# Pacing early weight loads, moving a quarter of the tail products, chaining late loads on one queue, and merging stores, in a two-branch attention kernel

## The chip, the cores and the metric

The kernel runs on one core of one Trainium2 chip. The metric is device time in microseconds (us). The kernel before took 2483.39 us (median of 4 runs, 2479.60 to 2484.12).

The names used below: TensorE does matrix products into PSUM, VectorE, ScalarE and GpSimd work on vectors, and SyncE here only issues DMA transfers. GpSimd issues some too. The profile calls TensorE's products PE, its weight loads PEld, and SyncE's queue SPq. SBUF is the memory that holds the weights loaded here, PSUM the one that the products are written to; a bank is one of the kernel's buffers there (eight in the tail). The granted clock is the share of full speed that TensorE was allowed (0.50 is half clock), the DMA share the mean busy share of the 16 DMA engines. A transfer is issued by a queue and lands when its completion is signalled. The drain is the end of the sliding branch, where TensorE runs short of work.

## The reference, cut to what matters

```python
x = A_x                                            # 2048 x 640
g = sigmoid((x * gate_w).sum(-1, keepdims=True))
a = sliding_window_attention(x, wqkv, wo)          # 32 heads of 20, window 256
# b: recurrent; 64 segments of 32 tokens, 8 memory tokens, 32 heads of 192
for s in range(64):
    h = concat(mem, x_s)                           # 40 x 640
    q, k, v = h @ Wq, h @ Wk, h @ Wv               # each 640 x 6144
    o = softmax(mask(q k^T)) v @ Wo
    mem, out_s = o[:8], o[8:]
return g * a + (1 - g) * b
```

The recurrent branch is sequential in `mem`, so it can't be spread. The queries, keys and values of a segment's own 32 tokens do not depend on `mem`. For the last eight of them the kernel computes these for all segments at once: these are the dense "tail" products. They run between the two branches.

## The kernel before

The matrices of the recurrent branch are cut into 84 units: 64 stay in SBUF (29 loaded early, 32 late, 3 last) and 20 are streamed in every segment from a packed copy in DRAM. The kernel records operations in a small list scheduler, which then emits instructions in the order of its own simulated clock. That clock decides only the order of each queue; the profile shows what an instruction then waited for: an input block's load that the scheduler counts as 500 ns held a product for 46.63 us.

```python
# (cut) early work of the sliding branch: to the scheduler these are free transfers
units  = [lambda sc, u=u: sc.op("DMA", 500, lambda: weights.load_resident(pre, u, nc.sync)) for u in early]
units += [lambda sc, u=u: sc.op("DMA", 500, lambda: weights.pack(u, nc.sync)) for u in streamed]
...
    # (cut) one output-weight unit is four transfers of 64 rows x 1280 bytes
    for r in range(2):
        i, b = divmod(2 * c + r, 3)
        for a in range(2):
            engine.dma_start(dst[64*a:64*a+64, r*D:(r+1)*D], self.Wo[8*g+2*i+a, 64*b:64*b+64, :])
...
# (cut) main
branch_A(..., units)                                  # sliding branch
for u in late: weights.load_resident(post, u, nc.gpsimd)      # 32 units at once
tail_projections(tc, weights, xTb, xbqk, xbv)         # dense products, 8 PSUM banks
for u in last: weights.load_resident(end, u, nc.gpsimd)
branch_B(...)                                         # recurrent branch
mix_out(...)
```

## Time and profile before

| stage | from, to (us) | length |
|---|---|---|
| sliding branch, with its stall | 0 to 435.8 | 435.8 |
| query and key products of the tail | 435.8 to 557.8 | 122.0 |
| value products of the tail | 557.8 to 615.2 | 57.4 |
| gap to the first recurrent product | 615.2 to 622.6 | 7.4 |
| first recurrent segment | 622.6 to 653.7 | 31.1 |
| the other 63 segments and the output mix | 653.7 to 2483.5 | 1829.8 |

The borders are the starts of the first and last products of a stage (so a stage's last product is cut off by its own length, some 0.3 us), and for a segment the copy of the new memory.

In the list of what TensorE waited for (us in total, times, longest us):

```profile
PE p_m L247 <- DMA a_xt<-in_A_x_dram: 59.1, 2, 46.6
...
PE t_psum L576 <- DVE t_qk L583: 12.5, 1, 12.5
```

The first is the stall for an input block. The second is TensorE's wait for the 26.66 us store of the chain.

### The profile page before, as it was taken

How to read it: one execution, taken by the hardware profiler on the slowest of the kernel's cores; microseconds unless marked ns; L12 is line 12 of the kernel's file. 1: busy time of each engine (PE TensorE's matmuls, PEld its weight loads, DVE VectorE, ACT ScalarE, POOL GpSimd, SP SyncE). 2: the span in 40 equal slices, each digit the busy share in tenths (PEclk: the TensorE clock that was granted, in tenths of full speed). 3: DMA queues.
4: the chain of work that ended last, by engine and by line, in shares of the span. 5: the costliest groups of instructions: out<-in, count | busy, mean ns of one | idle time of the engine just before them, and what ended most of it. 6: DMA issues, size and time to landing. Idle time of an engine off the chain costs nothing.

```text
span 2483.5 us, 112898 instructions
## 1 busy us (share of the span) xinstructions
PE 2129.7 (86%) x49059; PEld 1521.8 (61%) x49093; DVE 1133.4 (46%) x3942; ACT 1047.4 (42%) x2385; POOL 745.7 (30%) x2097
## 2 busy tenths in 40 slices
PE   2799997798888888888888888888888888888885
PEld 2477765795566665556666665565666666666664
DVE  2588885232344443334444444343443443444434
ACT  1588886122344333334433443333333333343333
POOL 2255554501322222222222222222222222222220
PEclk7899997899899999999999999999999999999997
DMA  9200000955788888878888887888887888888888
GB/s 327 61 21 27 27 19 9 298 148 140 246 276 272 272 275 265 255 246 267 274 270 272 278 270 253 259 280 264 264 267 251 264 266 280 270 273 263 269 260 244
DMA packets 298288, 561.55 MB, mean 226 GB/s; under 512 B 104568, under 2 KB 116864, under 8 KB 297792
## 3 DMA queue, kind: packets, MB, share of 16 engines
q1 hardware_dynamic: 273712, 513.01, 64.8%
q0 software_dynamic: 19808, 37.07, 5.2%
q8 instruction: 385, 6.31, 1.0%
q10 hardware_dynamic: 4272, 4.26, 0.6%
q14 instruction: 111, 0.91, 0.1%
HBM read 524.83 MB, written 36.51 MB: 226 GB/s over the span
## 4 chain that ended last, share of the span: by engine, by line
PE 56%; DMA 36%; ACT 3%; issue 2%; SPq 1%; DVE 1%; POOL 0%; ACTq 0%; DVEq 0%; POOLq 0%
DMA t_w<-w_packed 31%; PE ps_k L737 8%; PE ps_q L737 8%; PE ps_o L907 7%; PE ps_v L737 6%; PE t_psum L576 4%; PE p_s L326 3%; PE p_m L281 3%; PE ps_pv L883 2%; PE tr_k L752 2%; PE p_o L410 2%; PE S_ps L809 1%; PE t_psv L593 1%; PE p_st L326 1%; PE tr_q L752 1%
## 5 line engine op out<-in xcount | busy, mean ns | idle before, releaser
L737 PEld LDWEIGHTS <-t_hT 128*32 128x32 bf16 x15360 | 380.2, 98 | 286.7 <-issue 57.9
L907 PE MATMUL ps_o<-t_OT,t_w 128*128 128x40 bf16 x7040 | 289.3, 180 | 120.3 <-DMA t_w<-w_packed 111.9
L907 PE MATMUL ps_o<-t_OT,w_o 128*128 128x40 bf16 x8320 | 320.8, 180 | 47.2 <-ACT t_OT L888 45.2
L907 PEld LDWEIGHTS <-t_w 128*128 128x128 bf16 x7040 | 225.5, 96 | 141.7 <-DMA t_w<-w_packed 138.9
L907 PEld LDWEIGHTS <-w_o 128*128 128x128 bf16 x8320 | 267.1, 96 | 58.2 <-issue 48.4
L784 POOL COPY t_K<-t_xqk 128x64 bf16<-128x64 bf16 x256 | 60.9, 238 | 769.0 <-PE S_ps L809 763.6
L356 DVE CUSTOM_DVE_ANT_0 a_junk<-p_s,a_mask 128x384 bf16<-128x384 f32 (+2 forms) x512 | 253.5, 528 | 45.0 <-PE p_st L326 32.9
L386 ACT ACTIVATE a_pt<-p_st 128x384 bf16<-128x384 f32 (+2 forms) x512 | 220.4, 474 | 89.9 <-PE p_st L326 81.1
L737 PE MATMUL ps_v<-w_v,t_hT 128*32 128x384 bf16 x4864 | 252.9, 336 | 0.6 <-issue 0.6
L888 ACT CAST t_OT<-ps_pv 128x480 bf16<-128x480 f32 x256 | 143.2, 559 | 246.3 <-PE ps_pv L883 242.5
L737 PE MATMUL ps_q<-w_q,t_hT 128*32 128x384 bf16 x4096 | 220.0, 336 | 20.5 <-DVE t_hT L918 20.2
L775 DVE COPY t_K<-tr_k 128x256 bf16<-128x256 bf16 x256 | 74.6, 291 | 339.5 <-PE tr_k L752 339.1
L737 PE MATMUL ps_k<-w_k,t_hT 128*32 128x384 bf16 x4096 | 223.2, 339 | 0.6 <-issue 0.6
L742 ACT CAST t_tok<-ps_k 128x384 bf16<-128x384 f32 x256 | 122.7, 479 | 208.3 <-PE ps_k L737 208.3
L761 ACT COPY b_QT<-tr_q 128x384 bf16<-128x384 bf16 x256 | 123.3, 481 | 179.4 <-PE tr_q L752 179.4
L866 DVE TENSOR_TENSOR t_PTx<-PT_ps,mk_x 128x320 bf16<-128x320 f32 x256 | 125.9, 492 | 153.3 <-PE PT_ps L859 153.3
L394 POOL TENSOR_SCALAR_AFFINE_SELECT a_pt<-a_pt 128x512 bf16<-128x512 bf16 x240 | 148.0, 639 | 124.5 <-ACT a_pt L386 123.5
L742 ACT CAST t_tok<-ps_q 128x384 bf16<-128x384 f32 x256 | 122.6, 479 | 138.0 <-PE ps_q L737 137.6
L819 DVE TENSOR_REDUCE sm_mx<-S_ps 128x4 f32<-128x160 f32 x256 | 82.2, 321 | 204.4 <-PE S_ps L809 203.3
L742 ACT CAST t_vtok<-ps_v 128x384 bf16<-128x384 f32 x256 | 122.7, 479 | 103.0 <-PE ps_v L737 102.8
L697 POOL DMA_DIRECT2D t_xqk<-xbqk x256 | 137.4, 537 | 87.0 <-POOL b_QT L765 40.9
L326 PE MATMUL p_st<-a_qa,a_k 64*128 64x128 bf16 x1440 | 150.7, 224 | 10.6 <-ACT a_pt L386 7.3
(140 smaller groups left out, 4059.1 us busy)
## 6 DMA issues: line engine op xcount, KB each, us to landing
t_w<-w_packed SPq DMA_DIRECT2D x704, 320.0 KB, 4.2
t_w<-w_packed SPq DMA_DIRECT2D x576, 384.0 KB, 4.4
xbqk<-t_qk SPq DMA_DIRECT2D x16, 768.0 KB, 5.3
t_xqk<-xbqk POOLq DMA_DIRECT2D x256, 48.0 KB, 3.6
w_v<-in_B_Wv_dram POOLq DMA_DIRECT2D x19, 384.0 KB, 8.3
w_q<-in_B_Wq_dram SPq DMA_DIRECT2D x16, 384.0 KB, 7.3
xbv<-t_vt SPq DMA_DIRECT2D x64, 96.0 KB, 1.8
t_xv<-xbv POOLq DMA_DIRECT2D x128, 48.0 KB, 4.0
```

Of the source, the lines that this page charges most:

```text
L326: nc.tensor.matmul(T(out)[:, i * P:(i + 1) * P], lhsT=b if keys_first else a, rhs=a if keys_first else b, start=True, stop=True, tile_posi ...
L356: sc.op("DVE", 135 + n / 0.96, lambda: nc.vector.tensor_tensor_reduce(out=T(junk)[:, 0:n], in0=T(s)[:, 0:n], in1=mask[:, NKB * P - n:], op ...
L386: sc.op("ACT", act_ns(n), lambda: nc.scalar.activation(out=T(pt)[:, h % 4, 0:n], in_=T(s)[:, 0:n], func=ACT.Exp), reads=[s], writes=[pt])
L394: nc.gpsimd.affine_select(out=v, in_=v, compare_op=op, fill=0.0, base=0, pattern=[[0, 4], [sign, P]], channel_multiplier=-sign)
L576: nc.tensor.matmul(pt[:, bb, :], lhsT=ws[ki][kt][:, c:c + P], rhs=xTb[:, kt, t * P:(t + 1) * P], start=(kt == 0), stop=(kt == KT - 1))
L697: sc.op("DMA", 500, lambda: nc.gpsimd.dma_start(tile_of(qk)[:].rearrange("p i b t -> p (i b t)"), xbqk[s, :, g].rearrange("p i c -> p (i c ...
L737: nc.tensor.matmul(t[32 * j:32 * j + 32, 0:384], lhsT=tile_of(hT)[:, kt, :], rhs=w[:, j * 384:(j + 1) * 384], start=(kt == kts[0]), stop=( ...
L742: sc.op("ACT", act(384), lambda: nc.scalar.copy(tile_of(tok)[:], b["tile"][:, 0:384]), reads=[b], writes=[tok])
L761: nc.scalar.copy(dst, tq["tile"][:].rearrange("p b (j t) -> p b j t", t=SEG))
L866: nc.vector.tensor_tensor(out=tile_of(dst)[:], in0=PT["tile"][:, i, :, :].unsqueeze(2).to_broadcast([P, 2, 4, L]), in1=mk.unsqueeze(1).uns ...
L888: sc.op("ACT", act(480), lambda: nc.scalar.copy(tile_of(OT)[:].rearrange("p b j l -> p (b j l)"), o["tile"][:, 0:480]), reads=[o], writes= ...
L907: nc.tensor.matmul(t[:, dt * L:(dt + 1) * L], lhsT=w[:, r * D + dt * P:r * D + (dt + 1) * P], rhs=OT["tile"][:, b, i, :], start=(g == 0 an ...
```

## The change

The intent: stop the early loads from blocking the input blocks; fill the drain of the sliding branch with dense products; keep the late loads from crowding out the stores; and issue fewer, larger stores.

```diff
-    early, late, last = weights.resident[:29], weights.resident[29:-3], weights.resident[-3:]
+    early, late, last = weights.resident[:23], weights.resident[23:-2], weights.resident[-2:]
-    units = [... sc.op("DMA", 500, load_resident(pre, u, nc.sync)) for u in early]
-    units += [... sc.op("DMA", 500, pack(u, nc.sync)) for u in streamed]
+    units = [lambda sc, after, u=u: pack(sc, after, u) for u in streamed]          # now "SP", 1300
+    units += [lambda sc, after, u=u: sc.op("SP", 1300, load_resident(pre, u, nc.sync), after=after) for u in early]
 # in the sliding branch's loop: each unit follows a TensorE operation
-                units.pop(0)(sc)
+                units.pop(0)(sc, [o for o in sc.ops[-8:] if o["eng"] == "PE"][-1:])
 # after the sliding branch's last operation has been recorded
+        tail(sc)              # tail_qk of the first quarter, PSUM tag "m" (2 banks)
 # the tail has its own schedule now; late loads are chained on SyncE
+        for n, u in enumerate(late):
+            loads[u] = sc.op("SP", 1300, load_resident(post, u, nc.sync), after=[loads[late[n-1]]] if n else [])
+        for g in range(1, 4): tail_qk(...)
+        for g in range(4):    tail_v(...)
 # value stores: one for four PSUM tiles
-                    nc.sync.dma_start(xbv[h:h+2, tt*P:(tt+1)*P, :]..., vt[:])          # 64 x 96 KB
+        sc.op("SP", 1500, nc.sync.dma_start(xbv[8*g:8*g+8, tt*P:(tt+1)*P, :]..., view))  # 16 x 384 KB
 # (cut) the two "last" units load on SyncE inside the recurrent branch
```

More of the change, by code (lines that the diff above doesn't have):

```diff
@@ L137, in act_ns, with branch_A @@
     return 105 + n / 1.2
-def branch_A(tc, x, wqkv, wo, gate_w, spread_x, ga_dram, omg_dram, units, W=256, HA=32):
+def branch_A(tc, x, wqkv, wo, gate_w, spread_x, ga_dram, omg_dram, units, tail, W=256, HA=32):
     nc = tc.nc
@@ L159, in branch_A @@
               "rl": (2, [P, HH], FP32), "aT": (1, [P, KT, P], BF), "ga": (1, [P, D], BF), "zc": (1, col, FP32), "ez": (1, col, FP32),
-              "den": (1, col, FP32), "gcol": (4, col, FP32)}
+              "den": (1, col, FP32), "gcol": (4, col, FP32), "ts": (2, [P, P // MEM, 2, 12, MEM], BF), "w": (1, [P, 4 * 384], BF)}
         for i in range(2):
@@ L489, in branch_A @@
         for u in units:
-            u(sc)
+            u(sc, [])
         for _, u in queue:
             u()
+        tail(sc)
         with tc.manual_schedule():
@@ L552, in get, with tail_weights @@
         return t
-def tail_projections(tc, weights, xTb, xbqk, xbv):
+def tail_weights(sc, nc, weights, g, kinds, loads):
+    ws = {}
+    for u in [(k, g, kt) for k in kinds for kt in range(KT)]:
+        b = None
+        if u in weights.slot:
+            b = sc.buf("w")
+            sc.op("SP", 1300, lambda u=u, b=b: nc.sync.dma_start(sc.tile(b)[:, 0:weights.width(u)], weights.dram_of(u)), writes=[b], after=[loads.get(u)])
+        ws[u] = (b, loads.get(u), lambda u=u, b=b: sc.tile(b) if b else weights.tiles[u])
+    return ws
@@ new lines, in evacuate, with tail_qk, f @@
+def evacuate(sc, nc, n, ps, dst, out, src):
+    if n % 2:
+        sc.op("ACT", act_ns(512), lambda: nc.scalar.copy(out(), src()), reads=[ps], writes=[dst])
+    else:
+        sc.op("DVE", dve_ns(512), lambda: nc.vector.tensor_copy(out(), src()), reads=[ps], writes=[dst])
+def tail_qk(sc, nc, weights, xTb, xbqk, g, loads, after=()):
+    HS = P // MEM
+    ws = tail_weights(sc, nc, weights, g, "qk", loads)
+    for t in range(xbqk.shape[0] // HS):
+        st = sc.buf("ts")
+        for n in range(6):
+            kind, b4 = "qk"[n // 3], n % 3
+            ps, use = sc.buf("m"), [ws[kind, g, kt] for kt in range(KT)]
+            def f(ps=ps, use=use, b4=b4, t=t):
+                for bb in range(4):
+                    c = (4 * b4 + bb) * P
+                    for kt in range(KT):
+                        nc.tensor.matmul(sc.tile(ps)[:, bb * P:(bb + 1) * P], lhsT=use[kt][2]()[:, c:c + P], rhs=xTb[:, kt, t * P:(t + 1) * P],
+                                         start=(kt == 0), stop=(kt == KT - 1))
+            sc.op("PE", 20 * 56, f, reads=[u[0] for u in use if u[0]], writes=[ps], after=list(after) + [u[1] for u in use], name=("tail",), mode=128)
+            evacuate(sc, nc, n, ps, st, lambda st=st, n=n, b4=b4: sc.tile(st)[:, :, n // 3, 4 * b4:4 * b4 + 4, :].rearrange("p s b t -> p b s t"),
+                     lambda ps=ps: sc.tile(ps)[:].rearrange("p (b s t) -> p b s t", b=4, t=MEM))
+        sc.op("SP", 4000, lambda st=st, t=t: nc.sync.dma_start(xbqk[t * HS:(t + 1) * HS, :, g, :, :].rearrange("s p k c -> p s (k c)"),
+                                                               sc.tile(st)[:].rearrange("p s k b t -> p s (k b t)")), reads=[st])
@@ new lines, in tail_v, with f @@
+def tail_v(sc, nc, weights, xTb, xbv, g, loads):
+    ws = tail_weights(sc, nc, weights, g, "v", loads)
+    use = [ws["v", g, kt] for kt in range(KT)]
+    for tt in range(4):
+        st = sc.buf("ts")
+        view = lambda st=st: sc.tile(st)[:].rearrange("p s k b t -> p (s k b t)")[:, 0:1536]
+        for i in range(4):
+            ps = sc.buf("m")
+            def f(ps=ps, i=i, tt=tt):
+                for kt in range(KT):
+                    nc.tensor.matmul(sc.tile(ps)[:, 0:384], lhsT=xTb[:, kt, tt * P:(tt + 1) * P], rhs=use[kt][2]()[:, i * 384:(i + 1) * 384],
+                                     start=(kt == 0), stop=(kt == KT - 1))
+            sc.op("PE", 5 * 162, f, reads=[u[0] for u in use if u[0]], writes=[ps], after=[u[1] for u in use], name=("tail",), mode=128)
+            evacuate(sc, nc, i, ps, st, lambda view=view, i=i: view()[:, i * 384:(i + 1) * 384], lambda ps=ps: sc.tile(ps)[:, 0:384])
+        sc.op("SP", 1500, lambda view=view, tt=tt: nc.sync.dma_start(
+            xbv[8 * g:8 * g + 8, tt * P:(tt + 1) * P, :].rearrange("a t d -> t a d"), view().rearrange("p (a d) -> p a d", a=8)), reads=[st])
@@ L557, in tail_projections @@
+def tail_projections(tc, weights, xTb, xbqk, xbv, post, late):
     nc = tc.nc
-    nseg = xbqk.shape[0]
-    HS = P // MEM
     with ExitStack() as ctx:
-        ring = ctx.enter_context(tc.tile_pool(name="t_ring", bufs=3))
-        stage = ctx.enter_context(tc.tile_pool(name="t_stage", bufs=2))
-        vst = ctx.enter_context(tc.tile_pool(name="t_v", bufs=3))
-        ps = ctx.enter_context(tc.tile_pool(name="t_ps", bufs=8, space=bass.MemoryType.PSUM))
-        n = 0
-        for g in range(4):
-            ws = [[weights.get(ring, (kind, g, kt)) for kt in range(KT)] for kind in ("q", "k")]
-            for t in range(nseg // HS):
-                st = stage.tile([P, HS, 2, 12, MEM], BF, name="t_qk")
-                for ki in range(2):
-                    for b4 in range(3):
-                        pt = ps.tile([P, 4, HS * MEM], FP32, name="t_psum", tag="ps")
-                        for bb in range(4):
-                            c = (4 * b4 + bb) * P
-                            for kt in range(KT):
-                                nc.tensor.matmul(pt[:, bb, :], lhsT=ws[ki][kt][:, c:c + P], rhs=xTb[:, kt, t * P:(t + 1) * P],
-                                                 start=(kt == 0), stop=(kt == KT - 1))
-                        dst = st[:, :, ki, 4 * b4:4 * b4 + 4, :].rearrange("p s b t -> p b s t")
-                        src = pt[:].rearrange("p b (s t) -> p b s t", t=MEM)
-                        if n % 2:
-                            nc.scalar.copy(dst, src)
-                        else:
-                            nc.vector.tensor_copy(dst, src)
-                        n += 1
-                nc.sync.dma_start(xbqk[t * HS:(t + 1) * HS, :, g, :, :].rearrange("s p k c -> p s (k c)"),
-                                  st[:].rearrange("p s k b t -> p s (k b t)"))
-        for g in range(4):
-            ws = [weights.get(ring, ("v", g, kt)) for kt in range(KT)]
-            for tt in range(4):
-                for i in range(4):
-                    pt = ps.tile([P, 2, 192], FP32, name="t_psv", tag="ps")
-                    for kt in range(KT):
-                        nc.tensor.matmul(pt[:].rearrange("p a d -> p (a d)"), lhsT=xTb[:, kt, tt * P:(tt + 1) * P],
-                                         rhs=ws[kt][:, i * 384:(i + 1) * 384], start=(kt == 0), stop=(kt == KT - 1))
-                    vt = vst.tile([P, 2, 192], BF, name="t_vt")
-                    if n % 2:
-                        nc.scalar.copy(vt[:], pt[:])
-                    else:
-                        nc.vector.tensor_copy(vt[:], pt[:])
-                    n += 1
-                    h = 8 * g + 2 * i
-                    nc.sync.dma_start(xbv[h:h + 2, tt * P:(tt + 1) * P, :].rearrange("a t d -> t a d"), vt[:])
@@ new lines, in tail_projections, with make @@
+        shape = {"ts": (2, [P, P // MEM, 2, 12, MEM]), "w": (3, [P, WQ])}
+        pools = {t: ctx.enter_context(tc.tile_pool(name=f"t_{t}", bufs=n)) for t, (n, _) in shape.items()}
+        pools["m"] = ctx.enter_context(tc.tile_pool(name="t_ps", bufs=8, space=bass.MemoryType.PSUM))
+        def make(tag, n):
+            if tag == "m":
+                return pools[tag].tile([P, 512], FP32, name="t_psum", tag=tag)
+            return pools[tag].tile(shape[tag][1], BF, name=f"t_{tag}", tag=tag)
@@ L605, with branch_B @@
+        sc = Sched({"ts": 2, "w": 3, "m": 8}, make)
+        loads = {}
+        for n, u in enumerate(late):
+            loads[u] = sc.op("SP", 1300, lambda u=u: weights.load_resident(post, u, nc.sync), after=[loads[late[n - 1]]] if n else [])
+        for g in range(1, 4):
+            tail_qk(sc, nc, weights, xTb, xbqk, g, loads)
+        for g in range(4):
+            tail_v(sc, nc, weights, xTb, xbv, g, loads)
+        with tc.manual_schedule():
+            sc.run()
 STEP = "q0 k0 tq0 tk0 k1 q1 s0 tk1 tq1 v0 k2 q2 s1 tk2 k3 p0 tq2 q3 s2 pv0 v1 p1 o0 tq3 pv1 tk3 v2 p2 s3 o1 pv2 v3 p3 o2 pv3 o3"
-def branch_B(ctx, tc, xa_dram, xbqk, xbv, mem0, weights, xo_dram):
+def branch_B(ctx, tc, xa_dram, xbqk, xbv, mem0, weights, xo_dram, last):
@@ L701, in load_w @@
     def load_w(u):
+        if u in last:
+            loads[u] = sc.op("SP", 1300, last.pop(u), after=[o for o in sc.ops if o["eng"] == "PE"][8:9])
         if u not in weights.slot:
@@ L724, in branch_B @@
           writes=[hts[0][0]], after=[hts[0][1]])
-    made, tails = {}, {}
+    made, tails, loads = {}, {}, {}
     def chunk(kind, s, g):
@@ L911, in oproj @@
             sc.op("PE", 10 * 25.4, lambda c=c: f(c), reads=[OT] + [wb[c]] * (wb[c] is not None), writes=[o_b], name=("o", s, g, c),
-                  mode=128)
+                  mode=128, after=[loads.get(("o", g, c))])
         if g < 3:
@@ L1010, with pack @@
     weights = Weights(nc, dram, B_Wq, B_Wk, B_Wv, B_Wo, streamed)
-    early, late, last = weights.resident[:29], weights.resident[29:-3], weights.resident[-3:]
+    early, late, last = weights.resident[:23], weights.resident[23:-2], weights.resident[-2:]
     pre = ctx.enter_context(tc.tile_pool(name="b_pre", bufs=1))
-    units = [lambda sc, u=u: sc.op("DMA", 500, lambda: weights.load_resident(pre, u, nc.sync)) for u in early]
-    units += [lambda sc, u=u: sc.op("DMA", 500, lambda: weights.pack(u, nc.sync)) for u in streamed]
+    packs, xTb_ops = {}, []
+    def pack(sc, after, u):
+        packs[u] = sc.op("SP", 1300, lambda: weights.pack(u, nc.sync), after=after)
+    units = [lambda sc, after, u=u: pack(sc, after, u) for u in streamed]
+    units += [lambda sc, after, u=u: sc.op("SP", 1300, lambda: weights.load_resident(pre, u, nc.sync), after=after) for u in early]
     with tc.tile_pool(name="b_xtail", bufs=1) as xtail:
@@ L1026, in spread_x @@
                                                         sc.tile(xs)[:].rearrange("p s k t -> p s (k t)")), reads=[xs])
-            sc.op("POOL", 320, lambda: nc.gpsimd.tensor_copy(
+            xTb_ops.append(sc.op("POOL", 320, lambda: nc.gpsimd.tensor_copy(
                 xTb[:, :, qb * n * MEM:(qb + 1) * n * MEM].rearrange("p k (s t) -> p s k t", t=MEM),
-                sc.tile(xT)[:].rearrange("p k (s a t) -> p s a k t", s=n, t=MEM)[:, :, 3]), reads=[xT])
-        branch_A(tc, x, A_wqkv, A_wo, gate_w, spread_x, ga_dram[:], omg_dram[:], units)
+                sc.tile(xT)[:].rearrange("p k (s a t) -> p s a k t", s=n, t=MEM)[:, :, 3]), reads=[xT]))
+        branch_A(tc, x, A_wqkv, A_wo, gate_w, spread_x, ga_dram[:], omg_dram[:], units,
+                 lambda sc: tail_qk(sc, nc, weights, xTb, xbqk, 0, packs, xTb_ops[-1:]))
         post = ctx.enter_context(tc.tile_pool(name="b_post", bufs=1, side="right"))
-        for u in late:
-            weights.load_resident(post, u, nc.gpsimd)
-        tail_projections(tc, weights, xTb, xbqk, xbv)
+        tail_projections(tc, weights, xTb, xbqk, xbv, post, late)
     with ExitStack() as inner:
         end = inner.enter_context(tc.tile_pool(name="b_end", bufs=1))
-        for u in last:
-            weights.load_resident(end, u, nc.gpsimd)
-        branch_B(inner, tc, xa_dram, xbqk, xbv, mem0, weights, xo_dram)
+        branch_B(inner, tc, xa_dram, xbqk, xbv, mem0, weights, xo_dram, {u: lambda u=u: weights.load_resident(end, u, nc.sync) for u in last})
     mix_out(tc, xo_dram, omg_dram[:], ga_dram[:], outf)
```

## The prediction

> **What bounds the kernel now.** I read the page's 40 slices first, then a table of busy time by stage, then the chain of waits for the first 640 us, then the DMA issues of the SyncE queue. The kernel has four stages in time: the sliding branch (0 to 436 us), the dense tail projections (436 to 616), the recurrent branch (622 to about 2455) and the output mix. The change touches nothing in the last two except the first recurrent segment, and a comparison of the compiled instruction orders says that from the recurrent branch's first product on, TensorE runs the same sequence in both kernels. So some 1861 us (622.6 to the end) should only shift, and the prediction is about the first 623 us.
>
> Table by stage; columns: stretch and its length, then busy us (instructions) of PE, PEld, DVE, ACT, POOL, then granted clock, DMA share, GB/s:
> ```profile
> 40.00:75.00 35.00, 0.00 (x0) 0.00 (x0) 0.00 (x0) 0.00 (x0) 0.00 (x0) 0.50 0.66 206
> ...
> 80.00:85.00 5.00, 4.82 (x56) 2.65 (x55) 2.58 (x17) 2.39 (x10) 3.03 (x10) 0.79 0.25 67
> ...
> 200.00:300.00 100.00, 97.11 (x1852) 71.09 (x1857) 88.89 (x346) 84.67 (x196) 58.04 (x127) 1.00 0.08 23
> ```
> See that for 35 us no engine computes at all while the DMA engines are busy, and that in the steady sliding branch TensorE is the bound (97%) with the DMA engines nearly idle (8%). The timelines of SyncE's queue and of TensorE name the cause:
> ```profile
> 7.38 6.10 SPq L525 DMA_DIRECT2D w_q<-in_B_Wq_dram  x5
> ...
> 45.27 30.41 SPq L530 DMA_DIRECT2D w_packed<-in_B_Wo_dram  x44
> 75.80 0.51 SPq L232 DMA_DIRECT2D a_xt<-in_A_x_dram  x1
> ```
> ```profile
> 78.32 0.71 PE L247 MATMUL p_m<-a_ident,a_xt 128*128 128x128 bf16 x5 [46.63 <-DMA a_xt<-in_A_x_dram]
> ```
> The third input block is issued on SyncE only at 75.80, behind 29 early weight loads and all the packing copies; TensorE sat idle 46.63 us for it. Then the tail, from the chain of waits (start, length, what):
> ```profile
> 443.91 26.66 DMA xbqk<-t_qk
> 470.69 0.70 DVE t_qk L583
> 471.43 86.55 PE t_psum L576 x1520
> 557.98 33.36 PE t_psv L593 x205
> ```
> See the store that took 26.66 us beside a burst of late loads (its median landing is 5.3 us), then TensorE dense to 558 and through most of the value stage.
>
> [...]
>
> **The change part by part.**
>
> 1. *Early loads and packs paced over the sliding branch.* Removes the 46.63 us stall whole: three early loads still start first (the compiled SyncE order shows them ahead of the third input block), and they move 1.2 MB, some 4 us at the 327 GB/s of the first slice, against 16 us of slack before the block is needed at 31.7. It also removes the half-clock restart: 78.3 to about 82.1 ran at 0.5, so at most 1.9 us. Added work: 43 units of at most 384 KB, some 17 MB over 330 us, is 50 GB/s on DMA engines that are 8% busy, so hidden. TensorE's, VectorE's and ScalarE's orders in the sliding branch are instruction for instruction unchanged. Sum: −48.5, so the sliding branch ends near 387.3 instead of 435.8.
>
> 2. *First quarter of the dense products inside the sliding branch's schedule.* The intent is to fill the drain, where windows of 395 to 435 show TensorE busy 29.6 of 40 us, mostly at clock 0.50. I think it does not. The compiled order has all of the sliding branch's products first and the first dense product after its last output projection, exactly as before: the dense products take the same two-deep PSUM ring, whose places were dealt out in program order. So gain 0. Its cost is a boundary: the second scheduler's pools open only after the first's close, and the compiled waits show the first late load on SyncE waiting for all DMAs of the first part, the last big store included; the streamed weight that the next quarter's fifth product needs is issued right behind. From the quarter's last product: evacuation and semaphores 0.8, store issue 0.4, landing 4.2 (the minimum of these stores), two issues 0.8, landing of the second load behind the first about 4.8 (median for such weights 4.0 to 4.4). About 11 us idle, plus up to 1.9 for the half clock.
>
> 3. *Query and key products of the tail.* Before: 436 to 558, 122.2 us for 1920 products, which at 86.55/1520 = 0.0569 us need 109.3. So the 26.66 us store wait cost only 12.9 in all (the tile view shows TensorE idle 12.5 us for it), because eight PSUM banks let it run ahead. The paced late loads should remove this. After: 109.3 + start 0.7 + boundary 11 + restart 1.9 + 1.5 for streamed weights that arrive late between quarters = 124.4. Net +2: the wait is exchanged, not removed.
>
> 4. *Value products, 64 stores of 96 KB made 16 of 384 KB.* Before 57.7 us (557.8 to 615.5) for 320 products at 33.36/205 = 0.163 = 52.1. The same 384-byte rows move, so DMA time is equal; only waits go. Now late loads lie beside it: per 3.3 us about 1.9 us of store (share 0.55 before) and 1.2 us of load, 0.94 of the DMA engines, so I leave 3 us of waits: 55. Net −2.7.
>
> 5. *The start of the recurrent branch.* Before, its first weights and the memory vector were prefetched from 597 on, and from the last value product (615.5) to the first recurrent product (622.6) took 7.1. Now the compiled SyncE order puts six output-weight units, 24 issues, after the last value store and before the memory load. SyncE issues from DRAM to SBUF were 1.75 us for 4, so 24 take some 10.8. Evacuation 0.95 + store issue 0.4 + 10.8 + memory load 0.35 and 2.2 + transposes 0.6 = 15.3. Net +8.2. Two output-weight units (8 issues) also move into the first segment, which already waits for streamed weights: +2.
>
> Sum: −48.5 + 2 − 2.7 + 8.2 + 2 = −39, so 2483.85 − 39 = **2445 us**.
>
> **Rivals.** (a) *The drain is filled as intended*: up to 20 us more would go, 2425. For it speaks only the stated intent; the compiled order speaks against it. (b) *The boundary or the SyncE queue at the recurrent start hurts less*: with no boundary stall and a transition as before it would be 2445 − 13 − 8 = 2424; against it stand the compiled waits and the order of issues, which I trust more than my sizes. (c) *The DMA engines become the bound of the tail*: at 0.94 in the value stage a little worse packing stretches it by 5 to 10 us, 2450 to 2455. (d) *The stall is hidden anyway*: some of the 46.6 us could return as another wait in the sliding branch, as SyncE's order now has a packed weight's load waiting for its pack between input loads. But input blocks were loaded some 46 us ahead of use (issued 122.3, used 168), so a few us of blocking cost nothing.
>
> **Range and chances.** The stall's removal is nearly sure (47 to 50). The boundary (8 to 14), the value stage (52 to 60) and the transition (11 to 19, plus 0 to 4 in the first segment) are independent, some ±5 each; with a small tilt to less gain: 2432 to 2460. Two per cent faster needs 2434 or less, so nearly every estimate at its good end: 0.14. Slower by 2% would need a new 90 us wait: 0.01.
>
> **What would show it.** Right: TensorE busy near 97% from about 20 us on, without a hole at 32 to 78; the sliding branch ending near 387; the same drain at clock 0.50 just before; then 27 us of dense products, an idle of about 11 us ended by a streamed weight's load, 82 dense us; no 26 us store; the first recurrent product 14 to 17 us after the last value product, its releaser the memory load; and a distance of some 1863 us from there to the end. Wrong: dense products interleaved before 387 (a), no hole after the first quarter (b), gaps in the value stage ended by stores (c), or a recurrent branch that is itself longer or shorter by over 4 us, for which I have no cause.

The 1.9 us of half clock in part 1, and again in parts 2 and 3, are half of the 3.8 us (78.3 to about 82.1) that TensorE ran at half clock after the stall in the profile before. The same profile shows it after a shorter wait: in the 12.5 us of the store wait the granted clock fell from 1.00 (455 to 459) to 0.50 (465 to 474), and it was 1.00 again from 476, with products again from 471.4. That a waiting transfer on SyncE's queue holds back the one issued behind it was the author's estimate when the prediction was made; the result below measures it (a store landed at 416.96, the late load behind it was issued at 417.16, the streamed weight then took until 421.39).

## The result, and the profile after

The changed kernel took 2449.47 us (median of 4 runs, 2442.05 to 2458.99). The ratio to the kernel before is 0.987, 95% interval 0.983 to 0.991: 1.3% faster, so under 2%, as I had called likeliest. Ratios are the mean time of one kernel's fast runs over that of the other's of the same rounds, so not quite the ratio of the medians. The profiled run was the fastest, with a span of 2440.3 us.

| stage | before | after | difference | the prediction's term |
|---|---|---|---|---|
| sliding branch ends | 435.8 | 384.1 | −51.7 | −48.5 |
| query and key products | 122.0 | 120.3 | −1.7 | +2 |
| value products | 57.4 | 52.8 | −4.6 | −2.7 |
| gap to the recurrent branch | 7.4 | 21.3 | +13.9 | +8.2 |
| first segment | 31.1 | 30.6 | −0.5 | +2 |
| the rest | 1829.8 | 1831.1 | +1.3 | 0 |

The table by stage of the kernel after (columns as in the prediction's):

```profile
40.00:80.00 40.00, 39.30 (x675) 27.64 (x674) 35.23 (x153) 31.58 (x85) 17.57 (x42) 1.00 0.30 82
...
350.00:384.00 34.00, 27.93 (x327) 17.24 (x323) 10.03 (x37) 19.72 (x42) 12.77 (x23) 0.55 0.05 18
384.00:412.00 28.00, 27.66 (x480) 27.48 (x479) 8.07 (x13) 7.05 (x13) 0.00 (x0) 0.97 0.35 93
412.00:422.00 10.00, 0.95 (x10) 0.81 (x11) 0.46 (x1) 0.00 (x0) 0.00 (x0) 0.71 0.70 209
422.00:505.00 83.00, 82.73 (x1437) 82.37 (x1435) 24.89 (x36) 20.83 (x36) 0.00 (x0) 0.97 0.72 209
...
560.00:579.00 19.00, 0.65 (x13) 0.43 (x17) 0.18 (x1) 0.00 (x0) 4.15 (x23) 0.50 0.54 154
```

Read it from the top. Where no engine computed before (40 to 75), TensorE is now busy 39.3 of 40 us. The drain of the sliding branch (350 to 384) is untouched: clock 0.55, TensorE with holes. The first quarter of dense products, exactly 480, comes after it, not in it. Then come two new holes: 412 to 422 and 560 to 579. The chain of waits names the first, the timeline of SyncE's queue the second:

```profile
384.07 27.68 PE p_m L590 x480
411.77 0.70 DVE a_ts L573
412.52 4.44 DMA xbqk<-a_ts
...
417.16 0.35 SPq L527
417.50 0.05 issue
417.55 3.84 DMA t_w<-w_packed
```
```profile
557.30 2.56 SPq L532 DMA_DIRECT2D w_o<-in_B_Wo_dram  x4
559.98 0.52 SPq L614 DMA_DIRECT2D xbv<-t_ts  x1
560.54 15.31 SPq L532 DMA_DIRECT2D w_o<-in_B_Wo_dram  x24
575.95 0.46 SPq L754 DMA_DIRECT2D t_w<-in_B_mem_dram  x1
```

First hole: evacuation, landing of the quarter's last store (4.44), issue of a late load, landing of a streamed weight (3.84). Second hole: SyncE issues 24 output-weight loads in 15.31 us, 0.64 each, and only then the 10 KB of memory vectors with which the recurrent branch begins. The DMA share there is 0.54, and with the late output-weight loads on GpSimd's queue the gap fell from 21.3 to 6.6 us (the run is below), so the transfers were not the bound, their issue was. TensorE's waits after, against those shown of before, say the same (the 12.4 us left for the input are the very first block):

```profile
PE tp L759 <- DMA w_o<-in_B_Wo_dram: 20.4, 1, 20.4
...
PE p_m L248 <- DMA a_xt<-in_A_x_dram: 12.4, 1, 12.4
PE t_psum L590 <- DMA t_w<-w_packed: 8.7, 2, 8.4
```

The first line names the last output-weight load (it landed at 577.7). The product itself needs the memory vectors, issued just after that load; in the second profile of this kernel the same wait, 20.5 us, is put down to them.

The stall of 46.6 and the store wait of 12.5 are gone. In their place stand one wait of 8.4 and one of 20.4. Late loads, which ran on GpSimd's queue before, now stand on SyncE's ahead of what TensorE needs.

### The profile page after: what moved, and what is told of

Read it like the earlier page. It is cut to its first block, busy times and chain, and to the rows that moved or that the text cites. A ratio compares the mean times of both kernels' runs of the same rounds, so it can differ in the third digit from the quotient of the medians.

```text
span 2440.3 us, 112735 instructions
## 1 busy us (share of the span) xinstructions
PE 2134.8 (87%) x49093; PEld 1523.6 (62%) x49093; DVE 1130.5 (46%) x3942; ACT 1046.6 (43%) x2385; POOL 705.0 (29%) x2023
## 4 chain that ended last, share of the span: by engine, by line
PE 60%; DMA 33%; ACT 4%; issue 1%; SPq 1%; DVE 1%; POOL 0%; ACTq 0%; DVEq 0%; POOLq 0%
DMA t_w<-w_packed 31%; PE ps_o L946 8%; PE ps_k L776 8%; PE ps_q L776 8%; PE ps_v L776 6%; PE p_m L282 4%; PE p_s L327 3%; PE t_psum L590 3%; PE ps_pv L922 3%; PE tr_k L791 2%; PE p_o L411 2%; PE t_psum L610 2%; PE S_ps L848 1%; PE p_st L327 1%; PE tr_q L791 1%
## 5 line engine op out<-in xcount | busy, mean ns | idle before, releaser
L776 PE MATMUL ps_q<-w_q,t_hT 128*32 128x384 bf16 x4096 | 224.7, 342 | 18.7 <-DVE t_hT L957 18.4
```

The lines of the kernel that those rows point to most:

```text
L776: nc.tensor.matmul(t[32 * j:32 * j + 32, 0:384], lhsT=tile_of(hT)[:, kt, :], rhs=w[:, j * 384:(j + 1) * 384], start=(kt == kts[0]), stop=( ...
```

## The experiments

My theory after the result: the paced early loads give the whole gain (about 52 us), and the rest of the change loses about 8 of it again, in two places, by the order of transfers on one queue. The rivals are in the expectations. To compare the parts I use the **tail length**, from the first dense product to the first recurrent one, because the sliding branch itself ended either near 384 or at 386 to 390 from run to run: 186.8 us before, 194.5 after. The experiments ran on three chips, where the kernel before took 2503.16, 2507.23 (one run) and 2485.49 us. Kernels are compared only within the same rounds.

### The changed kernel and the kernel before, again

No edit. The changed kernel was profiled twice more, and the kernel before once more.

> The changed kernel once more, to see where its runs differ (2442 to 2459 us, while the kernel before kept within 5 us). Theory: the first 579 us are set by orders and issues and repeat within 2 us, so the spread lies in the recurrent branch, whose stream of weights runs with the DMA engines 84% busy: 2442 to 2459, and the stretch from the first recurrent product to the end differs from 1861.7 by as much as the total does. Rival: the spread comes from the tail, where loads and stores now share the queue: then the first recurrent product moves away from 578.6 by several us.

> The changed kernel again, as the reference of this call. First 579 us as before within 6 us; total 2440 to 2460 by the recurrent branch's chance of half-clock windows.

> The kernel before, with a profile on this chip, where its runs took 2490 to 2512 us instead of 2480 to 2484. Theory: its first 623 us are as in the first profile within 6 us, and the 62 recurrent segments are longer than 1768 us by 10 to 30, with more windows of half clock. Rival: the input-bound start or the tail is longer on this chip.

Measured, medians: 2450.71 against 2503.16 us for the kernel before of the same call (ratio 0.978, interval 0.973 to 0.983, unclear against the 2% line; a fourth run at 2485.36, over 1.5% above the fastest, counts as slow and is left out), and 2442.64 against 2485.49 (ratio 0.982, interval 0.979 to 0.985). With the first call that is three ratios between 0.978 and 0.987 for the same pair. In profile the tail length of the changed kernel is 194.5, 196.0 and 195.8, of the kernel before 186.8 and 186.5. The tail repeats, then, but the sliding branch does not: it ended at 384.1, 389.7 and 388.5, for a reason that no run isolates. So the first recurrent product came at 578.6, 585.7 and 584.3: the first repeat missed the 2 us that I had given it, the second kept within its 6. My theory that the spread lies in the recurrent branch failed for the first repeat: of its 8.7 us, 5.6 are the sliding branch, 1.5 the tail and only 1.6 the rest. The second profile of the kernel before was a single execution at a normal time (2482.24 us; first recurrent product at 623.0, against 622.6), on another chip than the slow runs, so it could not explain them.

### The paced early loads alone

```diff
 # the kernel before, with only the units changed; early 29, late 32, last 3 as before
-    units = [... sc.op("DMA", 500, load_resident ...) for u in early]
-    units += [... sc.op("DMA", 500, pack ...) for u in streamed]
+    units = [... sc.op("SP", 1300, pack ..., after=after) for u in streamed]
+    units += [... sc.op("SP", 1300, load_resident ..., after=after) for u in early]
```

> The kernel before with the first part alone: packs and early loads paced over the sliding branch (its 29 early units, its late loads, its tail and stores as before). Theory: the stall of 46.6 us and the half-clock restart go, 51 to 52 us in all, and nothing else moves: 2432 us, so faster than the whole change, whose other parts together cost 8 us or more. Rival: part of the gain of the whole change comes from its tail; then this alone gives 2440 to 2450.

Measured: the first recurrent product at 569.9 us, 52.7 earlier than before and 8.7 earlier than with the whole change; tail length 185.8, as before. TensorE again waited for the one store:

```profile
PE t_psum L576 <- DVE t_qk L583: 12.0, 1, 12.0
```

In total 2454.93 us (ratio 0.982, interval 0.977 to 0.987): 23 us over what I expected. The kernel before was slower by 20 us too, and in the profiled run (2450.53 us) the recurrent part accounts for the excess (62 segments took 1787.0 us, against 1768.4). So the stages say that this part alone gains more than the whole change; the totals, 2454.93 against 2450.71, do not tell the two apart.

### Late output weights on GpSimd's queue

```diff
-            loads[u] = sc.op("SP", 1300, ... load_resident(post, u, nc.sync) ...)
+            eng, q = ("POOL", nc.gpsimd) if u[0] == "o" else ("SP", nc.sync)
+            loads[u] = sc.op(eng, 2200 if u[0] == "o" else 1300, ... load_resident(post, u, q) ...)
```

> The changed kernel with the eleven late output-weight units issued on GpSimd's queue instead of SyncE's. Theory: the 21.0 us between the last value product and the first recurrent one is SyncE issuing 24 loads at 0.64 us ahead of the memory load; without them about 7 to 8 us, so 13 us less, 2436 us. Rival: the wait is for the last value stores to land and for GpSimd to set up its constants (at 563 to 567 us), so that at most 5 us go, or the GpSimd queue now delays its own loads and it gains nothing: 2445 to 2450.

Measured: the gap fell from 21.3 to 6.6 us, and the first recurrent product came at 566.2, 12.4 earlier. SyncE's issue was the cause. The next limit is the last value store: it landed at 563.2, and only then came the memory load (issued at 563.4) and GpSimd's constants (from 563.5), for which TensorE waits last:

```profile
PE tp L760 <- POOL ident masks.py:199: 5.7, 1, 5.7
```

The total, 2451.37 us, did not show it (expected 2436; the four runs lie between 2438.02 and 2469.72): this kernel's profiled run had the slowest recurrent branch of all (below).

### Filling the drain for real

```diff
 # tail_qk made a generator that yields after each PSUM group; in the sliding branch's loop:
+            if n > HA * NB + AUG:
+                next(fill, None)        # one dense group per step of the last block
-        tail(sc)
+        for _ in fill: pass
```

> The changed kernel with the 24 groups of dense products placed in program order among the last block's value products, ahead of its last output projection in the two-deep PSUM ring, so that the drain can really be filled. Theory: TensorE was busy only 28 of the 34 us from 350 to 384, at clock 0.55, so filled and at full clock the sliding branch and the first quarter end together 12 to 20 us earlier than 411.8: 2431 to 2438 us. Rival: the drain is bound by ScalarE's and GpSimd's chain of exponentials, and the dense products only push it later: under 5 us gained, 2445 or more.

Measured: the compiled order now interleaves dense products with the last block's attention, and the drain changes like this (table by stage, this kernel; the line of the changed kernel for the same stretch stands above):

```profile
350.00:384.00 34.00, 32.08 (x542) 27.43 (x541) 13.61 (x40) 15.98 (x33) 7.58 (x15) 0.83 0.19 49
```

TensorE was busy 32.1 us instead of 27.9, at clock 0.83 instead of 0.55. The sliding branch and the first quarter together ended at 403.8 instead of 411.7, 8 us earlier, between theory (12 to 20) and rival (under 5). The wait for a streamed weight that follows was 5.8 us instead of 8.4, so the last query and key product came at 493.9 instead of 504.4, 10.5 earlier. Both sizes are uncertain by some 5 us, as the sliding branch's end is. The end of the last block's attention still waits for GpSimd, VectorE and ScalarE in turn (1.23, 0.77 and 0.70 us in the chain of waits from 397 to 401; TensorE busy 6.7 of the 10 us from 395 to 405). The total, 2452.51 us against 2431 to 2438 expected, does not resolve it: the four runs lie between 2436.76 and 2472.58. The changed kernel had none of these 10.5 us, because its dense products came after the last output projection in a PSUM ring two deep.

### The first quarter back in the tail's own schedule

```diff
-    lambda sc: tail_qk(sc, nc, weights, xTb, xbqk, 0, packs, xTb_ops[-1:])
+    None
-        for g in range(1, 4):
+        for g in range(4):
             tail_qk(...)
```

> The changed kernel with the first quarter of the dense products back in the tail's own schedule (eight PSUM banks), the rest as changed. Theory: the boundary then lies between the sliding branch and the first dense product, where only small stores are outstanding and no streamed weight is needed for the first 3.4 us, so the idle of 9.7 us after the first quarter goes and at most 3 us come back: query and key products 113 to 117 us instead of 120.4, first recurrent product 5 to 8 us earlier. Rival: the idle is the unavoidable wait for the first streamed weights and only moves to another quarter: 120 us again.

This run and the next three are single executions, so their state is unknown (2434.09, 2461.59, 2429.24 and 2470.34 us in the order of the text); I read only their stages.

Measured: query and key products 113.9 us instead of 120.3, and a gap of 13.0 instead of 21.3, which I had not expected: the chain of late loads starts at 392.2 instead of 417.2, so only 12 loads instead of 24 were left for the end. The first recurrent product came at 568.8, 9.8 earlier. Tail length 178.8, which is 15.7 shorter than the changed kernel's. The boundary's cost is now one wait of 3.27 us:

```profile
389.97 4.58 PE L591 MATMUL t_psum<-xTb,w_q 128*128 128x128 bf16 x60 [0.59 <-DVE a_ga L452]
...
398.04 0.23 PE L591 MATMUL t_psum<-xTb,t_w 128*128 128x128 bf16 x1 [3.27 <-DMA t_w<-w_packed]
```

### Streamed weights of the second quarter loaded ahead

```diff
+    units += [lambda sc, after, u=u: ahead(sc, after, u) for u in (("q",1,4), ("k",1,4))]
 # tail_weights uses weights.ahead[u] for these two; for room:
-    early, late, last = resident[:23], resident[23:-2], resident[-2:]
+    early, late, last = resident[:21], resident[21:-4], resident[-4:]
```

> The changed kernel with the two streamed weights of the second quarter loaded during the sliding branch into tiles that live until the tail ends (two early units become late ones and two late ones load in the recurrent branch, for room). Theory: the idle of 9.7 us after the first quarter is the wait for the boundary's stores plus the streamed weight, and goes almost whole: query and key products 111 to 113 us. Rival: the boundary itself (freed pools, PSUM) holds TensorE: 5 us or more remain.

Measured: 110.8 us for the query and key products, so the hole went whole and the boundary itself holds nothing. But the room had to be paid for: with two more late loads in the chain, the value products waited 7.6 us for weights (62.5 us in all), and the first segment took 35.0 us. Tail length 190.0.

```profile
PE tp L763 <- DMA t_w<-in_B_mem_dram: 15.7, 1, 15.7
PE t_psum L614 <- DMA w_v<-in_B_Wv_dram: 7.6, 3, 5.7
```

### Late loads in one burst on GpSimd's queue, as before

```diff
-            loads[u] = sc.op("SP", 1300, ... nc.sync), after=[loads[late[n-1]]] if n else [])
+            loads[u] = sc.op("POOL", 600, ... nc.gpsimd))
```

> The changed kernel with its 39 late loads issued on GpSimd's queue at once, as in the kernel before, instead of chained on SyncE. Theory: the burst makes the store wait return in the second quarter (12 us of TensorE idle, as in the kernel before and in the run with the early loads paced alone), query and key products 130 to 135 us; and with no late loads on SyncE the gap before the first recurrent product falls to 7 to 9 us. So the first recurrent product moves by only -3 to +3 us. Rival: with the first quarter already done, the eight banks cover the burst: no more than 3 us lost in the products.

Measured: the store wait came back. The chain of waits shows a store of 29.41 us, and TensorE's list shows what of it counted:

```profile
421.90 29.41 DMA xbqk<-t_ts
```
```profile
PE t_psum L590 <- DVE t_ts L573: 15.3, 1, 15.3
```

Query and key products took 128.5 us (8.2 more than chained, a little less than the 10 to 15 expected), the gap 7.0. The 8.2 are a balance: the hole of 8.45 us after the first quarter is gone here, because no late load stands ahead of the streamed weights on SyncE's queue (they were issued from 385.4 to 387.2). Tail length 187.4, 7.1 shorter than the changed kernel's; the first recurrent product came 5.5 us earlier, where I had expected a move of 3 at most. So chaining the late loads on SyncE does prevent the store wait, as meant, and costs more, in the hole and at the end, than it saves.

### Small value stores

```diff
-        sc.op("SP", 1500, ... one store of 8 heads per four PSUM tiles)
+            sc.op("SP", 400, ... one store of 2 heads after each evacuation)   # same staging tile
```

> The changed kernel with the value stores as 64 of 96 KB from the same staging tiles. Theory: the stores' size is worth little while TensorE is dense, but their 48 more issues at 0.4 us fill SyncE beside 44 output-weight loads at 0.64: value products 54 to 57 us instead of 53.1 and first recurrent product 3 to 8 us later. Rival: the larger stores are what took the value products from 57.7 to 53.1: then they return to 57 or more whatever SyncE does, with the stores' landing as the releaser.

Measured: value products 58.3 us instead of 52.8, gap 25.5, tail length 205.4, 10.9 longer, more than the 3 to 8 that I had expected. Which side was right? TensorE's timeline has two waits in this stage, both for a weight and none for a store:

```profile
550.68 0.32 PE L610 MATMUL t_psum<-w_v,xTb 128*128 128x384 bf16 x1 [1.26 <-DMA w_v<-in_B_Wv_dram]
554.22 14.19 PE L610 MATMUL t_psum<-w_v,xTb 128*128 128x384 bf16 x76 [3.22 <-DMA w_v<-in_B_Wv_dram]
```

The timeline of SyncE's queue has four small stores between each of these loads and the next, so the weights were late. So in this kernel the larger stores are worth about 10 us, by freeing the queue. What they would be worth in the kernel before, where the loads ran elsewhere, no run tells.

### Two combinations

The first has the first quarter back in the tail and the late output weights on GpSimd's queue; the second has the filled drain, the two weights ahead, and the same queue. Their edits are those above.

> The changed kernel with its first quarter back in the tail's schedule and the late output weights on GpSimd's queue: the two losses that the runs showed, both undone. Theory: they add up, query and key products 114 us, value products 53, gap 7, so the first recurrent product near 558 (sliding branch at 384), 20 us earlier than the changed kernel's 578.6, and the time by as much shorter: 2425 to 2435. Rival: the gains overlap, because the earlier start of the late loads had already shortened the gap to 13: then 563 or later, 2435 or more.

> The drain filled, the second quarter's two streamed weights loaded ahead, and the late output weights on GpSimd's queue. Theory: filling takes 10 us, the loads ahead 9.5, the queue 13 to 14, less 4 us in the first segment for two more weights loaded there: first recurrent product near 548, 2420 to 2430 us. Rival: the value products wait for late weights as in the run with the loads ahead alone (62.5 us instead of 53), which takes 9 us back: 555 to 560, no better than the simpler version.

Measured with the changed kernel (2442.64 us):

| kernel | median of the runs | ratio to before, interval | tail length |
|---|---|---|---|
| changed kernel | 2442.64 | 0.982 (0.979 to 0.985) | 195.8 |
| first quarter back + GpSimd's queue | 2423.96 | 0.975 (0.971 to 0.978) | 172.4 |
| filled drain + weights ahead + GpSimd's queue | 2424.37 | 0.975 (0.972 to 0.978) | not comparable |

The first beats both kernels: 18.7 us under the changed one by the medians. Its gap is 6.6 and its query and key products take 113.9, so the two gains add up to 22 to 23 us of tail length, as the theory had it. The first recurrent product was at 562.3 rather than 558, since this run's sliding branch ended at 389.9. The second combination reached the recurrent branch earlier in absolute terms, at 555.9, as the rival said: the value products waited 7.8 us for weights again. It is no better in time than the simpler one.

### The recurrent branch varies by itself

From its first product on, TensorE's compiled order was compared with the kernel before for the changed kernel, the run with GpSimd's queue, the filled drain and both combinations: it is the same in all, and the traces agree but for some missing records. Yet the 62 middle segments took between 1750.5 and 1807.4 us. Table by stage over these segments, for the slowest and the fastest:

```profile
595.80:2403.20 1807.40, 1566.60 (x39184) 1090.63 (x39184) 734.96 (x2543) 675.26 (x1550) 481.42 (x1488) 0.96 0.83 261
```
```profile
595.10:2345.60 1750.50, 1546.90 (x39184) 1082.43 (x39184) 734.65 (x2543) 675.04 (x1550) 480.83 (x1487) 0.98 0.83 270
```

(First the run with late weights on GpSimd's queue, then the first combination.) The same number of products was busy 20 us longer at a mean clock of 0.96 instead of 0.98, and the other 37 us are waits. Divided into 31 pieces, the clock sits at 1.00 in some and at 0.97, 0.94 or 0.91 in others, at different places in each run. Of the 37 us of waits, 35.6 stand in one line of TensorE's list, the output products' wait for their streamed weight (us in total over the run, times, longest):

```profile
PE ps_o L947 <- DMA t_w<-w_packed: 132.2, 159, 2.5
```
```profile
PE ps_o L948 <- DMA t_w<-w_packed: 96.6, 154, 2.0
```

The traces also show which comes first, the waits or the half clock. The stretches of half clock, 38 in the slowest branch and 22 in the fastest, start on a grid of 3.41 us. In the 3.41 us before each of the 38, TensorE had been busy 35 to 74% of the time (median 53%); before the 450 grid steps at full clock the median is 91%, and only 6 of them are under 60%. (Steps that follow a half-clock one are left out.) The profile of the changed kernel shows the same over its 62 segments (609.2 to 2378.4 us): 27 stretches on that grid, TensorE busy 26 to 70% of the 3.41 us before each (median 55%), against a median of 92% before 458 steps at full clock, only 2 of them under 60%; its longest idle time there was 2.6 us. So in these profiles the idle time comes first, and the half clock follows it. Why the streamed weights came later in one run than in another (261 against 270 GB/s at the same DMA share of 0.83), no run settles. That is open.

## Why the prediction was right, point by point

- **Early loads paced: −48.5, measured −51.7** in the first profile and −46 to −47 in two later ones, −51.7 again in the run with this part alone. The mechanism was right and the size within its own spread.
- **The first quarter does not fill the drain: right**, shown by the order of the products in the profile and by the run that did fill it and gained 8 us there. The boundary was put at 11 us of idle and measured 9.3 (0.88 and 8.45 on TensorE); loading the weights ahead removed it, and so did taking the late loads off SyncE.
- **The store wait cost 12.9 us and not 26.66: right.** Bringing it back made TensorE wait 15.3 us. The net of this stage, +2 predicted, was −1.7, because the boundary was shorter, late streamed weights between the quarters cost 0.3 us instead of the 1.5 that I had allowed, and the products with start and half clock took 110.7 instead of 111.9.
- **Value products: −2.7 predicted, −4.6 measured.** Three us of waits beside a DMA share of 0.94 were allowed; the share was about 0.82 and TensorE waited 0.8 us. The rows of the stores cost the same, as assumed: packets of 384 bytes have a median of 22 ns in the DMA records of this stage in both profiles.
- **The gap: +8.2 predicted, +13.9 measured.** This is the term that was mis-sized most, and at 21.3 us the whole transition lay outside the 11 to 19 that I had given it. "24 take some 10.8" took the issue time from four loads of 128 rows (0.44 us each, which makes 10.5). The 64-row output loads took 0.59 and 0.04 between them: 15.3. A line that the prediction shows had the better figure: 44 packing copies of 64 rows in 30.41 us, 0.69 each. Some 1.5 us more, by my estimate from the timeline, are four further loads that held up the issue of the last value store (557.30 to 559.86). The mechanism, six units ahead of the memory load, was right to the instruction.
- **First segment +2: not settled.** It took 30.1 to 30.6 us in three profiles of the changed kernel, and 31.1 and 28.1 in the two of the kernel before. Loading four units there instead of two made it 35.0.
- **The rest shifts unchanged: right on the mean** (+1.3 in the first profile), but I gave its chance variation no room of its own. Over all profiles (1750.5 to 1807.4 us for the 62 segments) it is larger than any single term of the tail. That the sum held is in part luck: the errors of the terms nearly cancelled, −43.2 in the profile against −39, and the median of the timed runs lay 7 us above the profiled run.

## What to carry to other kernels

A transfer that costs nothing in a scheduler's clock is not free on its queue: the waits of 46.6 us before and of 20.4 us after were a small urgent transfer standing behind bulk ones on one queue, and the 8.4 us a streamed weight behind a load that itself had to wait for a store. One output-weight load is issued in 0.59 us and lands in a median of 2.5, but 24 of them took 15.31 us to issue one after another, at a DMA share of 0.54. So check for each queue what stands ahead of the first thing the next stage needs. A buffer ring dealt out in program order decided here where "filler" work could go (none of the drain filled as written, 8 us gained once the program order was changed); read the compiled order before believing that a gap is filled. Judge a change of 1% by the stages it touches, since a long stage that it does not touch may vary by more.
